# Scores of each batch moved behind its own k_m, the phi softmax one batch ahead, and its quotient folded into k_m and v_m

## Chip, cores and metric

The kernel runs on one core of a Trainium2 chip. The metric is the device time of one execution, in microseconds.

## What is computed

Linear-memory attention over 4 batches, 8 heads, 576 positions and head dimension 64, with 32 memory slots, and then two MLPs over its 2304 x 512 output:

```python
a = exp(phi - max(phi, over s)); a = a / (sum(a, over s) + 1e-9)      # [b,h,s,m]
k_m = einsum('bhsm,bhsd->bhmd', a, k);  v_m = einsum('bhsm,bhsd->bhmd', a, v)
scores = q @ k_m.T / sqrt(64); attn = softmax(scores, over m)
x = attn @ v_m                                       # 2304 x 512
x = (x @ w_a) * (x @ w_b) @ w_out                    # d_ff 1536
out = elu(x @ w_in) @ w2_out                         # d_ff 2048
```

The weights arrive as 64-bit words (float64). They are converted on the chip to a high and a low part, and every large product is done as three products of such parts.

## The kernel before

Everything is written out in program order for each engine (a manual schedule): an engine runs its instructions in the order in which the source emits them, and an instruction that waits holds everything behind it on its engine. SP's DMA queue and POOL's are in order too.

**Attention phase.** One loop over the 4 batches i. phi has 128 partitions (4 heads by 32 slots), two halves u, 576 positions. `a_max` (DVE maximum), `a_exp` (ACT exponential with a running sum) and `a_end` (DVE: add 1e-9, reciprocal, and the product with all of phi, L347) make the softmax over positions. `stage_aT` transposes it on PE into PSUM, and ACT copies it to `a_t` (L366, L369). `stage_kv` (L386) makes k_m (n=0) and v_m (n=1) of one half; `stage_m` (L393) copies the sum out of PSUM on ACT. `stage_turn` (L406) turns k_m and v_m into the layout that is needed next, `stage_kT` and `stage_vT` (ACT, L412, L417) copy that out. `stage_scores` (L426, L430) multiplies q with k_m; `stage_softmax` takes the maximum (L452) and the difference (L453) on DVE and the exponential on ACT (L454); `stage_norm` (L460 to L465, DVE) sums and divides; `stage_xT` (L473, L477) transposes on PE, and `split_sb` writes xhi on ACT (L69) and xlo on DVE (L70).

In iteration i the order is: the four `stage_kv` of batch i, norm of i-2, the end of phi's softmax of i+1, xT of i-2, turn of i, scores of i-1, six conversion pieces, aT of i+1, softmax of i-1, maximum and exponential of phi of i+2. So the scores of a batch run one iteration behind its k_m. The scores of batch 3 stand behind the loop, in the list `order` of the MLP phase, as do the xT of batches 2 and 3.

**Weights.** A unit is 128 x 512 words. `load_unit` brings it to one of three `raw` buffers, from SP's queue where `seq` says "unit", else from POOL's queue inside the third of seven conversion pieces. `magnitude` (L113) and `low_word` (L119) are two ACT passes over the raw unit; the seven pieces of a unit are DVE passes (L160 to L185) with a few ACT copies. `fill(n)` emits n pieces. In piece 4 and 5 of a unit the two ACT passes of the next unit are emitted, and they wait there for its load.

**Loads.** `seq` is the order in which SP loads phi (4 buffers), kv (6), left (2), q (4) and the units. `more_loads` issues from it until a buffer is not free; a stage that has read a buffer frees it and calls it again. k and v come as four transfers of 512 KB for each batch, q and phi as 1152 KB and 576 KB, left as 256 KB.

**MLP phase.** `step_u` (L497) multiplies v_m into w_a and w_b, so the first MLP's input need not be formed; its low part is a DVE pass (L507) deferred by one step. `steps_ab` (L590) multiplies attn with that, DVE multiplies the two results (L599), and ACT and DVE split the product (L600, L601). `steps_o1` (L632) follows, then the second MLP. Every step emits a share of the conversion pieces.

## Time and profile before

| | |
|---|---|
| median of 3 runs | 828.93 us (828.81 to 830.22) |
| the profiled execution | 829.17 us, span 827.4 us |
| PE busy | 790.7 us, 96% of the span |
| DVE busy | 593.1 us, 72% |
| ACT busy | 396.5 us, 48% |
| mean granted clock of TensorE | 0.984 |

The profiled execution's own time is 1.77 us longer than the span from its first to its last instruction. Busy shares are means over stages with different limits. In the views, idle time is put down to what ended it.

### The profile page before, as it was taken

What the parts mean: (1) busy time and instruction counts of PE and PEld (TensorE: products, weight loads), DVE (VectorE), ACT (ScalarE), POOL (GpSimd) and SP (SyncE); (2) the same over time, 40 slices, a digit from 0 to 9 for tenths busy, and PEclk for the clock granted to TensorE, in tenths of its full rate; (3) what the DMA queues carried; (4) which work ended last, traced back from release to release, by engine and by line L of the source; (5) the groups of instructions that cost most, each with busy time, mean ns of one, the idle gap of its engine ahead of it and who ended that gap; (6) DMA issues with size and microseconds to landing.
All of it is one profiled execution on the core that took longest, in us unless ns stands there. A gap on an engine that the chain in (4) does not pass through costs nothing.

```text
span 827.4 us, 14253 instructions
## 1 busy us (share of the span) xinstructions
PE 790.7 (96%) x6032; PEld 729.4 (88%) x6032; DVE 593.1 (72%) x979; ACT 396.5 (48%) x608; POOL 40.5 (5%) x87
## 2 busy tenths in 40 slices
PE   4588899999999999999999999999999999999997
PEld 3477789999999999999999899888999889998896
DVE  3488988678877886667778842787777786776464
ACT  2434576554434433343357754556654556553350
POOL 2000000000000000000000000000000000000000
PEclk9599999999999999999999999999999999999999
DMA  9882022112220221001000200111111110100006
GB/s 325 293 289 102 1 83 97 58 71 78 77 77 27 78 77 51 27 27 51 26 27 26 77 26 15 62 50 35 45 52 51 51 51 26 51 0 1 1 1 229
DMA packets 16815, 57.79 MB, mean 70 GB/s; under 512 B 1776, under 2 KB 1776, under 8 KB 16752
## 3 DMA queue, kind: packets, MB, share of 16 engines
q0 software_dynamic: 9360, 34.08, 11.7%
q1 hardware_dynamic: 7392, 22.81, 7.8%
q8 instruction: 47, 0.77, 0.4%
q14 instruction: 16, 0.13, 0.0%
HBM read 52.17 MB, written 4.72 MB: 69 GB/s over the span
## 4 chain that ended last, share of the span: by engine, by line
PE 91%; DVE 4%; ACT 2%; DMA 2%; issue 0%; SPq 0%; ACTq 0%; DVEq 0%
PE o_ps L776 24%; PE h_ps L733 24%; PE o_ps L632 18%; PE ab_ps L590 18%; PE u_ps L497 2%; PE sc L426 2%; DMA raw<-in_w_ab_dram 1%; PE pk L386 1%; DVE ssm L460 1%; DVE y L465 1%; PE tp_x L473 0%; PE tp_a L362 0%; DVE y L453 0%; DVE smx L452 0%; DMA phi_t<-in_phi_dram 0%
## 5 line engine op out<-in xcount | busy, mean ns | idle before, releaser
L590 PE MATMUL ab_ps<-xhi,u 128*128 128x288 f32 x768 | 139.4, 298 | 3.7 <-ACT xhi L69 2.9
L590 PEld LDWEIGHTS ab_ps<-xhi,u 128*128 128x128 f32 x768 | 114.1, 189 | 9.0 <-issue 3.2
L776 PE MATMUL o_ps<-ulh,g2h 128*128 128x512 f32 x288 | 113.7, 395 | 0.0
L776 PE MATMUL o_ps<-ull,g2h 128*128 128x512 f32 x288 | 113.6, 394 | 0.0
L776 PE MATMUL o_ps<-ulh,g2l 128*128 128x512 f32 x288 | 103.0, 395 | 0.0
L751 DVE SCALAR_TENSOR_TENSOR e<-e,th 128x768 f32<-128x768 f32 x48 | 46.0, 958 | 75.0 <-ACT e L748 74.6
L733 PE MATMUL h_ps<-yh,usl 128*128 128x384 f32 x384 | 97.8, 335 | 0.0
L733 PE MATMUL h_ps<-yl,ush 128*128 128x384 f32 x384 | 97.7, 335 | 0.0
L733 PE MATMUL h_ps<-yh,ush 128*128 128x384 f32 x384 | 97.7, 335 | 0.0
L744 ACT ACTIVATE e<-h_ps 128x768 f32<-128x768 f32 x48 | 39.0, 813 | 95.8 <-PE h_ps L733 93.6
L632 PE MATMUL o_ps<-gh,ulh 128*128 128x288 f32 x384 | 82.5, 296 | 0.6 <-DVE u L507 0.4
L632 PE MATMUL o_ps<-gl,ulh 128*128 128x288 f32 x384 | 82.2, 296 | 0.0
L632 PE MATMUL o_ps<-gh,ull 128*128 128x288 f32 x384 | 82.2, 296 | 0.0
L590 PE MATMUL ab_ps<-xlo,u 128*128 128x288 f32 x384 | 82.1, 295 | 0.0
L597 ACT ACTIVATE a_sb<-ab_ps 128x576 f32<-128x576 f32 x48 | 31.3, 652 | 86.4 <-PE ab_ps L590 86.4
L733 PEld LDWEIGHTS h_ps<-yh,ush 128*128 128x128 f32 x384 | 69.5, 188 | 1.3
L599 DVE TENSOR_TENSOR a_sb<-a_sb,ab_ps 128x576 f32<-128x576 f32 x48 | 36.1, 752 | 46.5 <-PE ab_ps L590 44.8
L733 PEld LDWEIGHTS h_ps<-yh,usl 128*128 128x128 f32 x384 | 69.4, 188 | 0.0
L733 PEld LDWEIGHTS h_ps<-yl,ush 128*128 128x128 f32 x384 | 69.3, 188 | 0.0
L776 PEld LDWEIGHTS o_ps<-ulh,g2l 128*128 128x128 f32 x288 | 54.0, 187 | 13.2
L776 PEld LDWEIGHTS o_ps<-ulh,g2h 128*128 128x128 f32 x288 | 54.0, 187 | 12.6
L776 PEld LDWEIGHTS o_ps<-ull,g2h 128*128 128x128 f32 x288 | 54.0, 187 | 12.5
(93 smaller groups left out, 1338.4 us busy)
## 6 DMA issues: line engine op xcount, KB each, us to landing
raw<-in_w_o_dram POOLq DMA_DIRECT2D x27, 512.0 KB, 3.5
raw<-in_w_ab_dram POOLq DMA_DIRECT2D x22, 512.0 KB, 3.6
kv_t<-in_kv_dram SPq DMA_DIRECT2D x16, 512.0 KB, 10.1
raw<-in_w_i_dram POOLq DMA_DIRECT2D x16, 512.0 KB, 3.6
y<-in_q_dram SPq DMA_DIRECT2D x8, 576.0 KB, 8.8
out_dram<-y SPq DMA_DIRECT2D x8, 512.0 KB, 2.9
phi_t<-in_phi_dram SPq DMA_DIRECT2D x3, 576.0 KB, 11.8
left_t<-in_kv_left_dram SPq DMA_DIRECT2D x4, 256.0 KB, 12.1
```

Of the source, the lines that this page charges most:

```text
L386: nc.tensor.matmul(pk[M * h:M * h + M, D * u:D * u + D], a[0:P if j < NJ else LEFT, u, j, M * h:M * h + M], rows, start=(j == 0), stop=(j ...
L426: nc.tensor.matmul(sc[:, u, j * P:(j + 1) * P], qs[u][:, t, j * P:(j + 1) * P], kt[:, u, t * P:(t + 1) * P], start=(t == 0), stop=(t == 1))
L460: nc.vector.tensor_reduce(out=sm, in_=at, op=ALU.add, axis=AX.X)
L497: nc.tensor.matmul(ps[j:j + M, o, k * 256:k * 256 + 256], vt[r, 2 * k + c, 2 * p + o], w[r, c * 256:c * 256 + 256], start=True, stop=True, ...
L590: nc.tensor.matmul(ps[:, h, 0:HS], u[:, kk, w, n * P:n * P + P], x[b][:, kk, h * HS:(h + 1) * HS], start=(kk == 0 and i == 0), stop=(kk == ...
L597: nc.scalar.activation(out=a_sb, in_=ps[:, :, 0:HS], func=AF.Copy)
L599: nc.vector.tensor_tensor(out=a_sb, in0=a_sb, in1=ps[:, :, 0:HS], op=ALU.mult)
L632: nc.tensor.matmul(ps[:, h, 0:HS], w[:, cc], g[:, h * HS:(h + 1) * HS], start=(n == 0 and i == 0), stop=(n == len(fs) - 1 and i == 2),)
L733: nc.tensor.matmul(ps[:, h, 0:HB], w[:, c], x[:, c, h * HB:(h + 1) * HB], start=(c == 0 and i == 0), stop=(c == KC - 1 and i == 2),)
L744: nc.scalar.activation(out=e, in_=ps[:, :, 0:HB], func=AF.Relu, scale=-1.0)
L751: nc.vector.scalar_tensor_tensor(out=e, in0=e, scalar=1.0, in1=th, op0=ALU.add, op1=ALU.mult)
L776: nc.tensor.matmul(ps[:, k, :], g[:, c * P:(c + 1) * P], w, start=(f == fs[0] and i == 0), stop=(f == fs[-1] and i == 2),)
```

## The change

Batch i's scores now run in iteration i, behind its own turn, with aT of i+1 (or the first `step_u`) on PE between the turn and the scores. phi's maximum, exponential and reciprocal of batch i+2 are done in iteration i. The product with all of phi is gone; the reciprocal is instead the scale of the ACT copy that takes k_m and v_m out of PSUM, which becomes two copies of 64 columns each. The exponential of the scores is a stage of its own, emitted one iteration later, behind the first `stage_m`; norm and xT of i-1 run in iteration i. The list `order` loses the scores of batch 3, and some of its entries change places. The two ACT passes of a unit are emitted right ahead of its first piece until iteration 1 is over, and only then one unit ahead. Conversion pieces are emitted as 7 in iteration 0 (behind `stage_vT`), and 7 in each of the iterations 1 to 3 (ahead of norm). In `seq`, q of a batch now follows its own kv and the phi ahead of it, and precedes the kv of the next batch.

```diff
@@ -93,7 +93,7 @@
...
     live = {False: 0, True: 0}
-    state = {"loaded": 0, "n": 0, "slot": 0}
+    state = {"loaded": 0, "n": 0, "slot": 0, "ahead": False}
     def load_unit(eng=nc.gpsimd):
         n = state["loaded"]
@@ -108,13 +108,13 @@
     def magnitude(n):
-        if n < NU:
+        if n < NU and "a" not in cu[n]:
             a = conv.tile([P, 512], U32, tag="a", name="a", bufs=2)
             nc.scalar.activation(out=a.bitcast(F32), in_=cu[n]["h"].bitcast(F32), func=AF.Abs, scale=65536.0)
             cu[n]["a"] = a
     def low_word(n):
-        if n < NU:
+        if n < NU and "lw" not in cu[n]:
             t = conv.tile([P, 512], BF16, tag="lw", name="lw", bufs=2)
             nc.scalar.activation(out=t, in_=cu[n]["l"], func=AF.Copy, scale=2.0 ** -52)
             cu[n]["lw"] = t
@@ -150,6 +150,9 @@
...
         whole = n < NU
+        if whole and slot == 0:
+            magnitude(n)
+            low_word(n)
         a = cu[n]["a"] if whole else None
         if slot == 1 and not to_hi(n - 1):
             return False
@@ -173,10 +176,12 @@
...
             cu[n]["p2"] = p2
-            low_word(n + 1)
+            if state["ahead"]:
+                low_word(n + 1)
         elif whole and slot == 5:
             nc.vector.tensor_tensor(out=cu[n]["lw"], in0=cu[n]["lw"], in1=cu[n]["p2"], op=ALU.mult)
-            magnitude(n + 1)
+            if state["ahead"]:
+                magnitude(n + 1)
         elif whole and slot == 6:
             to = a.bitcast(F32)
             if whole_words(n):
@@ -210,7 +215,7 @@
...
-    FILLS = 6, 6, 6, 6
+    FILLS, FILLS2 = (0, 7, 7, 7), (0, 0, 0, 0)
     RATE_AB, RATE_U, RATE_O1 = 1.0, 1.0, 3.0
     RATE_H, RATE_O2 = 2.5, 3.0
     ORDER, ORDER_H, ORDER_O2 = "0f1a2", "fa0bf1c2", "0f1fa2"
@@ -305,14 +310,12 @@
     NPHI, NQ, NKV = 4, 4, 6
-    seq = [("phi", 0, (0,)), ("phi", 0, (1,)), ("left", 0), ("kv", 0, 1, 0), ("kv", 0, 1, 1),
-           ("kv", 0, 0, 0), ("kv", 0, 0, 1), ("unit",), ("phi", 1)]
-    for b in range(1, B):
+    seq = [("phi", 0, (0,)), ("phi", 0, (1,))]
+    for b in range(B):
         seq += [("left", b)] + [("kv", b, n, u) for n in (1, 0) for u in range(2)]
         seq += [("unit",)] if b < 3 else []
-        seq += [("phi", b + 1)] if b + 1 < B else []
-        seq += [("q", b - 1, 0), ("q", b - 1, 1)]
-    seq += [("q", B - 1, 0), ("q", B - 1, 1)]
+        seq += [("phi", x) for x in ((1, 2), (3,), (), ())[b]]
+        seq += [("q", b, 0), ("q", b, 1)]
     free = {"phi": NPHI, "q": NQ, "kv": NKV, "left": 2}
     loads = {"phi": load_phi, "q": load_q, "kv": load_kv, "left": load_left, "unit": lambda: load_unit(nc.sync)}
@@ -336,20 +339,14 @@
     def a_exp(b, u):
         t = st["phi", b][:, u]
-        sm = p0.tile([P, 1], F32, tag="sm", name="sm", bufs=3)
+        sm = p0.tile([P, 1], F32, tag="sm", name="sm", bufs=4)
         nc.scalar.activation(out=t, in_=t, func=AF.Exp, bias=st.pop(("nm", b, u)), accum_out=sm)
         st["sm", b, u] = sm
     def a_end(b, u):
-        t, sm = st["phi", b][:, u], st.pop(("sm", b, u))
+        sm = st["sm", b, u]
         nc.vector.tensor_scalar(out=sm, in0=sm, scalar1=1e-9, scalar2=None, op0=ALU.add)
         nc.vector.reciprocal(out=sm, in_=sm)
-        nc.vector.tensor_scalar(out=t, in0=t, scalar1=sm, scalar2=None, op0=ALU.mult)
...
-    def stage_a(b, u):
-        a_max(b, u)
-        a_exp(b, u)
-        a_end(b, u)
     def stage_aT(b, us=(0, 1)):
         t = st["phi", b]
@@ -390,7 +387,9 @@
     def stage_m(b, n):
         t = st["m", n, b] = p0.tile([P, 2, D], F32, tag="m", name="m", bufs=2)
-        nc.scalar.activation(out=t, in_=st.pop(("pk", n, b))[:, 0:2 * D].rearrange("p (u d) -> p u d", u=2), func=AF.Copy)
+        pk = st.pop(("pk", n, b))
+        for u in range(2):
+            nc.scalar.activation(out=t[:, u], in_=pk[:, D * u:D * u + D], func=AF.Copy, scale=st["sm", b, u])
     def stage_turn(b, n):
@@ -451,7 +450,11 @@
...
             nc.vector.tensor_tensor(out=at, in0=ps, in1=mx.to_broadcast(list(at.shape)), op=ALU.subtract)
-            nc.scalar.activation(out=at, in_=at, func=AF.Exp, scale=SCALE)
...
+    def stage_exp(b):
...
+        for (at, _, _), n in zip(st["at", b], (P, LEFT)):
+            nc.scalar.activation(out=at[0:n], in_=at[0:n], func=AF.Exp, scale=SCALE)
     def stage_norm(b):
@@ -522,57 +525,61 @@
...
         more_loads()
-        stage_a(0, 0)
-        stage_aT(0, (0,))
-        stage_a(0, 1)
-        stage_aT(0, (1,))
-        magnitude(0)
-        low_word(0)
-        fill(2)
+        for u in range(2):
+            a_max(0, u)
+            a_exp(0, u)
+            stage_aT(0, (u,))
+        for u in range(2):
+            a_end(0, u)
         for i in range(B):
...
                 stage_m(i, n)
-            if i == 0:
-                fill(4)
-                a_max(1, 0)
-                a_max(1, 1)
-                a_exp(1, 0)
-                a_exp(1, 1)
-            if i > 1:
-                stage_norm(i - 2)
-            if i + 1 < B:
-                a_end(i + 1, 0)
-                a_end(i + 1, 1)
-            if i == B - 1:
-                step_u(0, 0, 0)
+                if n and i:
+                    stage_exp(i - 1)
+            fill(FILLS[i])
+            if i:
+                stage_norm(i - 1)
+            else:
+                for u in range(2):
+                    a_max(1, u)
+                    a_exp(1, u)
+                for u in range(2):
+                    a_end(1, u)
             tick()
-            if i > 1:
-                stage_xT(i - 2)
             stage_turn(i, 1)
             stage_turn(i, 0)
             stage_kT(i)
             stage_vT(i)
-            if i == B - 1:
+            if i == 0:
+                magnitude(0)
+                low_word(0)
+                fill(7)
+            if i + 1 < B:
+                stage_aT(i + 1)
+            else:
                 es_l.close()
                 es_p.close()
                 pb = es_b.enter_context(tc.tile_pool(name="pb", bufs=2, side="right", reuse_waits="tile"))
                 pss.append(ctx.enter_context(tc.tile_pool(name="ps2", bufs=2, space=PSUM, reuse_waits="tile")))
-            if i:
-                stage_scores(i - 1)
-            fill(FILLS[i])
-            if i + 1 < B:
-                stage_aT(i + 1)
-            if i:
-                soft_tiles(i - 1)
-                stage_softmax(i - 1)
-            if i + 2 < B:
-                a_max(i + 2, 0)
-                a_max(i + 2, 1)
-                a_exp(i + 2, 0)
-                a_exp(i + 2, 1)
+                step_u(0, 0, 0)
+            stage_scores(i)
+            tick()
+            for u in range(2 if i + 2 < B else 0):
+                a_max(i + 2, u)
+                a_exp(i + 2, u)
+            fill(FILLS2[i])
+            soft_tiles(i)
+            stage_softmax(i)
+            for u in range(2 if i + 2 < B else 0):
+                a_end(i + 2, u)
+            state["ahead"] = i > 0
+            if i and i + 1 < B:
+                stage_xT(i - 1)
+        stage_exp(B - 1)
...
         def steps_ab(f, b, amount):
             u = u_t.pop((f, b))
             a_sb = pb.tile([P, 2, HS], F32, tag="a_sb", name="a_sb", bufs=3)
@@ -657,15 +664,8 @@
...
-        def last_scores():
-            stage_norm(last - 1)
-            stage_scores(last)
-            soft_tiles(last)
-            stage_softmax(last)
...
-        order = [("ab", 0, 0), ("do", last_scores), ("ab", 0, 1), ("u", 1, 0), ("u", 0, 1),
-                 ("do", lambda: stage_xT(last - 1)), ("ab", 1, 0), ("do", lambda: stage_norm(last)), ("ab", 0, 2),
+        order = [("ab", 0, 0), ("do", lambda: stage_xT(last - 1)), ("u", 1, 0), ("ab", 0, 1), ("u", 0, 1),
+                 ("do", lambda: stage_norm(last)), ("ab", 1, 0), ("ab", 0, 2),
                  ("do", lambda: stage_xT(last)), ("ab", 1, 1), ("u", 1, 1), ("ab", 0, 3), ("ab", 1, 2),
                  ("u", 2, 0), ("u", 2, 1), ("ab", 1, 3)]
         for f in range(2, NF1):
```

## Rows read from the trace of the kernel before

**Rows 1.** Windows by stage: busy us of each engine, PEclk granted clock, DMA share, GB/s.

```profile
18.84:29.69 10.85, 0.00 (x1) 0.00 (x1) 3.00 (x8) 2.95 (x9) 0.53 (x1) 0.55 1.03 378
45.60:75.87 30.27, 25.03 (x513) 20.95 (x513) 26.44 (x49) 14.28 (x31) 0.53 (x1) 1.00 0.57 194
75.87:113.28 37.41, 33.42 (x325) 30.79 (x325) 33.35 (x57) 18.58 (x30) 1.59 (x3) 1.00 0.09 29
145.00:827.40 682.40, 677.83 (x4472) 630.17 (x4470) 488.24 (x785) 326.42 (x462) 29.48 (x53) 1.00 0.14 49
```

**Rows 2.** Chain that ended last, 0 to 30 us: start, us, what.

```profile
14.49 12.22 DMA raw<-in_w_ab_dram
```

**Rows 3.** Timeline of ACT: start us, us, engine, line, op, out<-in [idle before <-releaser].

```profile
26.74 0.66 ACT L119 ACTIVATE lw<-raw 128x512 bf16<-128x512 uint32 x1 [8.77 <-DMA raw<-in_w_ab_dram]
...
27.84 0.76 ACT L340 ACTIVATE phi_t<-phi_t,nm 128x576 f32<-128x576 f32 x1
...
38.54 0.28 ACT L393 ACTIVATE m<-pk 128x128 f32<-128x128 f32 x1 [2.48 <-PE pk L386]
...
86.21 1.36 ACT L454 ACTIVATE y<-y 128x1024 f32<-128x1024 f32 x2 [6.84 <-DVE y L453]
```

**Rows 4.** Timeline of PE, same columns.

```profile
18.20 0.64 PE L406 MATMUL pt<-y,m 128*64 128x128 f32 x8
29.69 1.97 PE L362 MATMUL tp_a<-ident,phi_t 128*128 128x128 f32 x8 [10.85 <-DVE sm L345]
...
39.92 5.65 PE L426 MATMUL sc<-y 128*128 128x128 f32 x32
...
48.79 0.65 PE L386 MATMUL pk<-kv_t,a_t 128*32 128x64 f32 x32 [0.95 <-ACT a_t L366]
...
53.59 1.07 PE L473 MATMUL tp_x<-ident,y 128*128 128x128 f32 x8 [1.42 <-DVE y L465]
...
55.67 3.84 PE L426 MATMUL sc<-y 128*128 128x128 f32 x32
...
60.46 1.09 PE L362 MATMUL tp_a<-ident,phi_t 128*128 128x128 f32 x8
...
75.87 0.53 PE L590 MATMUL ab_ps<-xhi,u 128*128 128x288 f32 x2
...
79.17 3.73 PE L426 MATMUL sc<-y 128*128 128x128 f32 x32
...
93.41 0.50 PE L590 MATMUL ab_ps<-xhi,u 128*128 128x288 f32 x2 [2.92 <-ACT xhi L69]
```

**Rows 5.** Timeline of SP's queue: start us, us, line, transfer issued.

```profile
4.29 0.61 SPq L103 DMA_DIRECT2D raw<-in_w_ab_dram  x1
...
19.32 0.34 SPq L293 DMA_DIRECT2D y<-in_q_dram  x1
```

**Rows 6.** DMA issues at 4.29 and 19.32 us: KB, us from issue to landing.

```profile
raw<-in_w_ab_dram SPq DMA_DIRECT2D x1, 512.0 KB, 12.1
...
y<-in_q_dram SPq DMA_DIRECT2D x1, 576.0 KB, 13.2
```

**Rows 7.** Timeline of DVE, columns as in rows 3.

```profile
29.93 0.52 DVE L347 TENSOR_SCALAR phi_t<-phi_t,sm 128x576 f32<-128x576 f32 x1
...
70.94 0.68 DVE L168 SCALAR_TENSOR_TENSOR a<-raw,a 128x512 uint32<-128x512 uint32 x1
...
73.65 0.43 DVE L163 TENSOR_SCALAR a<-a 128x512 uint32<-128x512 uint32 x1
...
80.11 1.53 DVE L460 TENSOR_REDUCE ssm<-y 128x32 f32<-128x1024 f32 x2
...
83.71 1.21 DVE L452 TENSOR_REDUCE smx<-sc 128x32 f32<-128x1024 f32 x1
...
86.88 0.41 DVE L173 TENSOR_SCALAR p<-a 128x512 uint16<-128x512 uint16 x1
...
93.19 1.23 DVE L70 TENSOR_TENSOR xlo<-tp_x,xhi 128x1024 fp32r<-128x1024 f32 x1
```

## The prediction

> **What bounds the kernel now.** I read the windows by stage first [rows 1]. From 145 us to the end PE is busy 677.83 of 682.40 us, so nothing there can give much; the change must be judged in the first 113.28 us, up to the first product of `steps_o1`. Between 75.87 and 113.28 us PE is busy 33.42 of 37.41 us. The large hole is 18.84 to 29.69 us: PE does nothing, and TensorE's granted clock falls.

> The chain of waits names the hole [rows 2]: the raw unit that SP issued at 14.49 us lands 12.22 us later. The timeline of ACT shows why weights stop the attention [rows 3]: the `low_word` of unit 1 waits for that unit until 26.74, and the exponentials of phi(1) at 27.84 stand behind it in ACT's queue. PE starts aT(1) at 29.69 and finds the clock at half: scores(0) take 5.65 us on L426, scores(1) only 3.84 [rows 4].

> The DMA is full meanwhile (share 1.03) [rows 1], so what comes next is the landing of the data. Unit 0, the 3392nd KB of SP's order, lands at 4.29 + 12.1 = 16.4 us, and q(0)'s second half, the 8512th (KB of 1024 bytes), at 19.32 + 13.2 = 32.5 [rows 5, 6]. With one unit of POOL's between them that is (8512 - 3392 + 512) / 16.1 = 350 KB/us.

> **The change: reference point.** All work from the first o1 product on is the same in both kernels. So the new time is 829.17 - (113.28 - T1), where T1 is when PE gets there now. I follow PE, with each wait that could be last.

> **Loads, new order.** From 16.4 us and KB 3392 at 350 KB/us: phi(1) 18.1, phi(2) 19.7, q(0) 23.0, the four kv(1) 25.2 to 29.6, unit 1 31.0, phi(3) 32.7, q(1) 36.0, kv(2) 38.2 to 42.6, unit 3 44.1; one POOL unit (1.5 us more), q(2) 48.9, kv(3) to 55.5; another POOL unit, q(3) 60.3. SP issues some 12 us ahead, and the buffers that it waits for (kv, left, q) come free earlier than that, so I take the DMA as never starved. Bounds: the mean up to unit 0 is (3392 + 512) / 14.4 = 271 KB/us, which puts q(3) at 16.4 + 15296 / 271 = 72.8; the upper end is the hole's 378 GB/s, 369 KB/us [rows 1], q(3) at 57.9.

> **Batch 0.** Without L347 (0.52 us each on DVE [rows 7]) aT(0) starts a little earlier. This saving I cost at nothing: phi(1) lands at 18.1 anyway. Its two maxima and two exponentials, with the 1.9 us from the first exponential to PE [rows 3, 4], put aT(1) at about 20. PE has then been idle some 3 us and I take the low clock: aT 2.5 us, to 22.6. q(0) is there at 23. Scores at the half clock for 4 us (before, they rose to the full clock after about 4 us of L426), then full: to 28.9 us.

> **Batch 1.** kv at full clock takes 53.59 - 1.42 - 48.79 = 3.4 us [rows 4]; the last kv(1) is needed at 31.5 and lands at 29.6. So to 32.3. `stage_m` is now two copies with a scale, which the trace does not show; one 128-column copy takes 0.28 us [rows 3], so two halves lie between 0.28 and 0.56; I take 0.44, nearer to two fixed costs; the extra 0.16 counts four times between kv and turn, 0.6 us. [...]

> From here DVE is the tightest engine. Prices [rows 7]: six pieces of a unit 3.2 us (70.94 to 73.65, and 0.43), norm 3.6 (80.11 to 83.71), the DVE part of softmax 3.2 (83.71 to 86.88), xlo 1.35, two maxima 1.3, the rest of `a_end` 0.75. Pieces of unit 1 start when ACT has made its magnitude, behind m(1,0), at 33.5: to 36.7; norm(0) 40.3; maxima of phi(3) 41.6; softmax(1) 44.8; `a_end` 45.5; xlo(0) 46.9. On PE meanwhile turn and aT(2) to 34.9, scores(1) to 39.8 (q(1) 36.0 is in time), xT(0) waits for norm(0), 40.3 to 41.7, kv(2) to 45.1.

> **Batches 2 and 3.** DVE: pieces of unit 2 to 50.0, norm(1) 53.6. PE: turn to 46.9, aT(3) 48.2; kT(2) is behind four conversion passes on ACT, 48.7; scores(2) 48.9 to 53.8 with q(2); xT(1) to 55.2; kv(3), with the last transfer at 55.5, to 58.7. ACT's m, two passes, kT and vT to 61.5; `step_u` 62.5; scores(3) (4.8 us from first product to the next stage [rows 4]) 62.5 to 67.4. DVE's pieces, norm(2) and u's low part end near 66.5, so softmax(3) follows at once, to 70. I take 68 for the first `steps_ab`, rounded up for waits of some tenths that I did not count.

> **To T1.** Before, from 75.87: 33.42 us of PE work [rows 1], of which scores(3), here already done, are 4.7; 28.7 remain. Before there are 3.99 us of idle: 2.92 of it is PE at 93.41 waiting for xhi, because ACT had stood 6.84 us at the exponential of batch 3 [rows 3, 4]. In the new order that exponential is before the phase, so that stall goes. What is late next: the low part of the second `step_u` is deferred by one step and is now emitted behind norm(3). DVE runs from 70 through pieces, L599, xlo(2), two low parts and norm(3) to about 83.7 and gives that low part at 85.9; PE, with 3.3 us for each `steps_ab` (75.87 to 79.17 [rows 4]), wants it at 82.2. That is a stall of 3.7 us; bounds 0 (DVE less late) and 6. T1 = 68 + 28.7 + 3.7 = 100.4.

> **Sum.** 829.17 - (113.28 - 100.4) = 816.3 us in the profiled execution's terms; the median of the runs was 0.24 lower, so **816 us**.

> **Rivals.**
> *The clock stays low longer.* For: at 18.84 PE idle brings it down, and between 29.69 and 39.92 us the aT and kv products did not bring it back. Against: it stays full through later gaps of 1 to 1.5 us [rows 1, 4]. Low through kv(1) and scores(1) adds 2.2 + 0.7 + 1.9, about 5 us: 821. [...]

> *The loads set the end.* With 271 KB/us scores(3) start at 72.8 instead of 62.5: 826. This is also the way to **slower**: q(b) is now needed in its own iteration, where before it had a batch of slack. From scores(3) starting at 75.9 us on, that is below 15296 / 59.5 = 257 KB/us, the kernel is slower than before; at 240 it is 833. Against: the hole's rate is 378 GB/s with all queues full [rows 1].

> *More is won.* The clock is back early in scores(0) (2 us) and DVE gives the low part in time (3.7 us): 810.5.

> *It does nothing.* What is won is given back because DVE, busy 33.35 of 37.41 us before T1 [rows 1], holds PE in the first MLP: 829. For it speaks that conversions are only shifted; against it, that DVE loses L347 and stood idle 7.85 of the hole's 10.85 us, so that there is room for its work to move forward.

> **How the numbers follow.** A measurement here tells about 0.2% (1.7 us). Forecast 0.62 (811 to 821); low clock or slow loads, still faster, 0.17 (821 to 827); more won 0.12; nothing 0.03; slower 0.06. The range 810 to 824 leaves out a third of the second (above 824), half of the third (below 810) and the last two, together 0.2. Faster 0.91, same 0.03, slower 0.06.

> **What would show it.** The wait of ACT for the raw unit near 14 to 27 us is gone, and PE has no hole over 4 us after aT(1). The last q lands near 60 us; the first `steps_ab` starts near 68, the first o1 product near 100. DVE has next to no idle from 33 to 70 us. A stall on `ab_ps` behind norm(3), put down to DVE's L507, near 82 us. From T1 on the two timelines run the same. I am wrong if q(2), q(3) or kv(3) land more than 5 us late, if the granted clock stays at half beyond 30 us, or if PE's idle after T1 grows by more than 2 us.

## The result, and the profile after

The changed kernel took 815.45 us (median of 4 runs, 814.24 to 816.64), the kernel before 828.87 us beside it (4 runs, 827.61 to 830.22): a ratio of 0.9838, with a 95% interval of 0.9812 to 0.9863. The forecast was 816 us, range 810 to 824. The profiled execution took 816.60 us, with a span of 814.8.

The windows of the changed kernel come first, for four stretches (columns as in [rows 1]).

```profile
0.00:30.00 30.00, 17.01 (x346) 13.28 (x347) 12.16 (x28) 13.24 (x32) 5.12 (x23) 1.00 0.96 346
...
30.20:36.00 5.80, 5.80 (x77) 4.72 (x77) 2.31 (x5) 2.35 (x8) 0.34 (x1) 0.50 1.03 307
...
48.32:84.13 35.81, 31.71 (x458) 26.99 (x457) 34.42 (x62) 18.59 (x36) 1.58 (x3) 1.00 0.31 120
...
100.63:814.80 714.17, 708.44 (x4794) 658.32 (x4792) 518.57 (x837) 349.35 (x513) 32.54 (x59) 1.00 0.15 51
```

From the first o1 product on nothing changed: 714.17 us here, 827.4 - 113.28 = 714.12 before [rows 1, 4]. So the whole gain lies ahead of that product, which moved from 113.28 to 100.63 us. The chain of waits no longer holds a weight unit of 12.22 us, as in [rows 2]; at its start now stands the second half of q(0), issued at 7.64 us and landed 14.09 us later, for which PE waits 0.66 us. What PE waited for in all is this (the view of waits; us in total, times, longest):

```profile
PE tp_a L359 <- ACT phi_t L343: 9.2, 3, 5.9
PE pk L383 <- issue: 4.1, 2, 2.8
PE ab_ps L597 <- DVE u L510: 3.0, 2, 2.7
PE o_ps L639 <- DVE u L510: 1.6, 1, 1.6
PE sc L425 <- ACT y L411: 0.8, 1, 0.8
PE sc L425 <- DMA y<-in_q_dram: 0.7, 1, 0.7
```

The hole of 10.85 us ahead of aT(1) [rows 4] has become 1.87. The second entry is new: "issue" means that PE waited for nothing that the profile shows. The timeline of PE says where it was:

```profile
17.32 1.42 PE L359 MATMUL tp_a<-ident,phi_t 128*128 128x128 f32 x8 [1.87 <-ACT phi_t L343]
...
21.87 2.02 PE L425 MATMUL sc<-y 128*128 128x128 f32 x16 [0.66 <-DMA y<-in_q_dram]
...
26.73 0.65 PE L383 MATMUL pk<-kv_t,a_t 128*32 128x64 f32 x30 [0.16 <-PE pk L383]
30.19 0.37 PE L383 MATMUL pk<-kv_t,a_t 128*32 128x64 f32 x2 [2.82 <-issue]
...
35.98 4.04 PE L425 MATMUL sc<-y 128*128 128x128 f32 x32
...
46.34 0.55 PE L383 MATMUL pk<-kv_t,a_t 128*32 128x64 f32 x25 [1.27 <-issue]
...
47.07 0.45 PE L405 MATMUL pt<-pair,m 128*64 128x64 f32 x8
...
50.26 3.84 PE L425 MATMUL sc<-y 128*128 128x128 f32 x32 [0.79 <-ACT y L411]
...
66.65 0.53 PE L597 MATMUL ab_ps<-xhi,u 128*128 128x288 f32 x2
...
84.18 1.16 PE L597 MATMUL ab_ps<-xhi,u 128*128 128x288 f32 x4 [2.68 <-DVE u L510]
...
100.63 0.43 PE L639 MATMUL o_ps<-gh,ulh 128*128 128x288 f32 x2
```

The first of these holes splits a group of 32 products of one tile, whose data were there, into 30 and 2, the second one into 7 and 25. DVE, by its timeline:

```profile
33.48 0.43 DVE L163 TENSOR_SCALAR a<-a 128x512 f32<-128x512 f32 x1 [5.79 <-ACT a L113]
...
48.32 0.43 DVE L163 TENSOR_SCALAR a<-a 128x512 f32<-128x512 f32 x1 [1.60 <-ACT a L113]
...
67.62 1.21 DVE L451 TENSOR_REDUCE smx<-sc 128x32 f32<-128x1024 f32 x1
...
82.92 1.21 DVE L510 TENSOR_TENSOR u<-u_ps,u 128x1024 fp32r<-128x1024 f32 x1
```

From 48.32 us, the first piece of unit 2, to 84.13, the end of u's low part, DVE is busy 34.42 of 35.81 us. PE's stall ends 0.05 us behind it.

### The profile page after: what moved, and what is told of

The parts are those of the page before. It is cut to its first block, busy times and chain, and to the rows that moved or that the text cites. A ratio compares the mean times of both kernels' runs of the same rounds, so it can differ in the third digit from the quotient of the medians.

```text
span 814.8 us, 14254 instructions
## 1 busy us (share of the span) xinstructions
PE 790.4 (97%) x6032; PEld 728.1 (89%) x6032; DVE 589.4 (72%) x971; ACT 398.7 (49%) x616; POOL 40.3 (5%) x87
## 4 chain that ended last, share of the span: by engine, by line
PE 91%; DVE 4%; DMA 2%; ACT 1%; issue 1%; SPq 0%; DVEq 0%
PE o_ps L776 25%; PE h_ps L733 25%; PE o_ps L639 19%; PE ab_ps L597 18%; PE u_ps L500 2%; DMA y<-in_q_dram 2%; PE pk L383 1%; PE sc L425 1%; DMA kv_t<-in_kv_dram 1%; DVE u L510 0%; DVE y L468 0%; DVE ssm L463 0%; DVE y L452 0%; DVE smx L451 0%; DVE gl L608 0%
## 5 line engine op out<-in xcount | busy, mean ns | idle before, releaser
L606 DVE TENSOR_TENSOR a_sb<-a_sb,ab_ps 128x576 f32<-128x576 f32 x48 | 36.1, 753 | 47.3 <-PE ab_ps L597 46.9
L776 PEld LDWEIGHTS o_ps<-ulh,g2l 128*128 128x128 f32 x288 | 54.0, 187 | 13.2
L776 PEld LDWEIGHTS o_ps<-ulh,g2h 128*128 128x128 f32 x288 | 54.0, 187 | 12.7
## 6 DMA issues: line engine op xcount, KB each, us to landing
raw<-in_w_ab_dram SPq DMA_DIRECT2D x3, 512.0 KB, 12.3
```

Of the source, the lines that this page charges most:

```text
L606: nc.vector.tensor_tensor(out=a_sb, in0=a_sb, in1=ps[:, :, 0:HS], op=ALU.mult)
L776: nc.tensor.matmul(ps[:, k, :], g[:, c * P:(c + 1) * P], w, start=(f == fs[0] and i == 0), stop=(f == fs[-1] and i == 2),)
```

## The experiments

My theory: the weight passes and the load order win the start of the phase together, and from then on DVE's chain sets T1. The rival: PE's own chain, with its clock and its holes, or the loads set T1 all along. X stands for the start of unit 2's first piece on DVE (48.32 in the changed kernel).

**b_unit_late**: the kernel before, with the two ACT passes of a unit emitted late until iteration 1 is over, and the six conversion pieces of iteration 0 behind aT(1).

```diff
...
+        if whole and slot == 0:
+            magnitude(n)
+            low_word(n)
...
-            fill(FILLS[i])
+            if i:
+                fill(FILLS[i])
             if i + 1 < B:
                 stage_aT(i + 1)
+            if i == 0:
+                fill(FILLS[i])
+            state["ahead"] = i > 0
```

> The kernel before, with one thing changed: in iterations 0 and 1 the two ACT passes over a raw unit stand right ahead of its first piece, and iteration 0's six pieces behind aT(1), so no exponential of phi stands behind a unit's load. Theory 'the unit's wait is the first of several limits': the exponentials of phi(1) run near 19 to 20 us and kv(1) ends near 32 instead of 38.4, but scores(0) then wait for q(0), which lands at 32.5 in this load order; about 6 of the 10.85 us come out, 822 to 823.5 us. Rival 'the wait was the whole loss': all 10 us come out, 818 to 819. Rival 'the hole only moves': 828 to 829.

Measured: 825.45 us (823.85 to 828.61, 10 runs) beside 829.25, ratio 0.9963 (0.9949 to 0.9978). aT(1) starts at 20.21 and the first o1 product at 107.91 in the profiled execution. The weights did stop the attention, but freeing it alone gives about 4 us (5.4 at the first o1 product of the profiled execution, the fastest of the ten), less than the 6 us that the theory expected.

**b_fold**: the kernel before, with the quotient folded into `stage_m` (and more buffers for the sums `sm`).

```diff
...
-        nc.vector.tensor_scalar(out=t, in0=t, scalar1=sm, scalar2=None, op0=ALU.mult)
...
+        for u in range(2):
+            nc.scalar.activation(out=t[:, u], in_=pk[:, D * u:D * u + D], func=AF.Copy, scale=st["sm", b, u])
```

> The kernel before with the fold alone: no product with phi on DVE (8 times 0.52 us), the reciprocal as scale of two 64-column copies. Theory: hidden, since the unit's load still sets when PE goes on; three later batches lose up to 0.5 us of DVE each and gain 0.24 us of ACT each (two copies 0.52 us against 0.28): 827.5 to 829.5. Rival 'the fold is the gain': 8 times 0.52 us on the path, 825 or less.

Measured: 828.62 us (828.14 to 831.76, 10 runs), ratio 0.9994 (0.9985 to 1.0004). PE still stands 10.29 us ahead of aT(1). The fold alone is worth nothing there. What it is worth in the new order was not run: of the products that it saves, those with phi(2) and phi(3) would fall into stretches where DVE waits anyway (5.79 and 1.60 us, ahead of 33.48 and 48.32 us), but that is argued.

**a_old_loads**: the changed kernel with the old list of loads.

```diff
-    seq = [("phi", 0, (0,)), ("phi", 0, (1,))]
-    for b in range(B):
+    seq = [("phi", 0, (0,)), ("phi", 0, (1,)), ("left", 0), ("kv", 0, 1, 0), ("kv", 0, 1, 1),
+           ("kv", 0, 0, 0), ("kv", 0, 0, 1), ("unit",), ("phi", 1)]
+    for b in range(1, B):
...
+        seq += [("q", b - 1, 0), ("q", b - 1, 1)]
+    seq += [("q", B - 1, 0), ("q", B - 1, 1)]
```

> The changed kernel with the old list of loads alone. Theory 'the order of the loads is needed by the new order of the stages': scores(0) cannot start before q(0)'s landing near 32 us (19.2 and 21.9 with the new list), later q's stand behind kv transfers that wait for buffers; the first steps_ab start near 74 to 77 instead of 66.65, 822 to 826 us. Unit 0 lands again near 16.4 us, not 14.1, if what is queued behind it (left(1)) slows it. Rival 'DVE sets the pace anyway': 815 to 817.

Measured: 830.49 us (828.71 to 833.23, 10 runs), ratio 1.0023 (1.0010 to 1.0036): slower than before, 15 us above the changed kernel, and beyond the 822 to 826 us that the theory expected. The timeline of SP's queue shows why (start, us, transfers issued):

```profile
17.18 1.83 SPq L298 DMA_DIRECT2D y<-in_q_dram  x2
...
21.00 15.38 SPq L308 DMA_DIRECT2D kv_t<-in_kv_dram  x4
...
37.38 0.90 SPq L298 DMA_DIRECT2D y<-in_q_dram  x2
...
38.89 18.78 SPq L308 DMA_DIRECT2D kv_t<-in_kv_dram  x4
57.72 1.95 SPq L298 DMA_DIRECT2D y<-in_q_dram  x4
```

The timeline of PE in the same execution:

```profile
27.81 5.74 PE L427 MATMUL sc<-y 128*128 128x128 f32 x32 [6.53 <-DMA y<-in_q_dram]
...
46.70 3.75 PE L427 MATMUL sc<-y 128*128 128x128 f32 x16 [6.48 <-DVE nm L339]
...
64.26 3.81 PE L427 MATMUL sc<-y 128*128 128x128 f32 x32 [2.74 <-DMA y<-in_q_dram]
```

Scores(0) wait 6.53 us for q(0), which stands behind the four kv(1) in the old list and is issued only at 17.18 (at 6.58 with the new list). PE cannot read kv(1) before these scores, and a kv buffer comes free only when PE has read it: so the four kv(2) take 15.38 us to issue, where they took this long with the new list:

```profile
25.34 4.93 SPq L308 DMA_DIRECT2D kv_t<-in_kv_dram  x4
```

q(1) and q(2) stand behind kv(2) and kv(3) in the same queue, and scores(1) and scores(2) wait for them 6.48 and 2.74 us (the first is listed under a maximum that DVE had done by 27.7 us; q(1), issued at 37.38, landed 9.2 us later). The new place of the scores thus needs the new list: without it, the change loses what the weight passes won. The new list without the new place was not run.

**a_norm_late** and **norm_late_again**: the changed kernel with the norm of batch 3 one step later, first beside the kernel before, then beside the changed kernel.

```diff
-                 ("do", lambda: stage_norm(last)), ("ab", 1, 0), ("ab", 0, 2),
+                 ("ab", 1, 0), ("do", lambda: stage_norm(last)), ("ab", 0, 2),
```

> The changed kernel with norm(3) emitted behind steps_ab(1,0) instead of ahead of it. Theory: the 2.68 us that PE waits for u's low part behind norm(3), and the half clock from 84.2 to 87.4 us that follows it (about 1.4 us), go; xT(3) may wait up to 1 us for norm(3): 811.5 to 813.5. Rival 'DVE is the bound and the wait only moves': 815 to 816.5.

> The changed kernel with the norm of batch 3 behind the first steps_ab of half 1 once more, now beside the changed kernel itself. If the stall of 2.68 us on u's low part is on the path that sets the end, it is about 2 us faster than the changed kernel (813.4 against 815.5). If the difference seen before was the scatter of the early phase, it is under 1 us.

Measured: 813.35 us (812.33 to 815.12, 4 runs), ratio 0.9809 (0.9793 to 0.9825), and again 812.63 us (812.19 to 812.96, 4 runs), ratio 0.9800 (0.9786 to 0.9815). The stall on u's low part is gone, and PE waits at xT(3) for the norm instead (timeline of PE in norm_late_again; 1.43 us in a_norm_late):

```profile
84.23 1.06 PE L476 MATMUL tp_x<-ident,y 128*128 128x128 f32 x8 [1.42 <-DVE y L468]
```

This version is faster than both kernels. In the profiled executions X to T1 took 50.19 and 49.45 us, where the changed kernel took 52.31 and, in the run that follows, 51.00. X came at 47.20 and 46.95 us, up to 1.4 us sooner than in the changed kernel; the edit lies behind X, so that part is not shown to be its work.

**after_again**: the changed kernel once more.

> The changed kernel once more, as the reference for the three kernels beside it on the same chip. Every theory expects 814.2 to 816.6 us. The question is only how far the time and the first product of steps_ab scatter when nothing is changed.

Measured: 817.43 us (814.78 to 818.78, 4 runs), ratio 0.9854 (0.9831 to 0.9877). So the eight runs of the changed kernel lie between 814.24 and 818.78, wider than expected. All four of norm_late_again, on the same chip, lie below. The timeline of PE in the profiled execution, which is the fastest of these four, shows one source of the spread; what made the others slower is not known:

```profile
83.93 0.80 PE L597 MATMUL ab_ps<-xhi,u 128*128 128x288 f32 x4 [2.69 <-DVE u L510]
...
84.83 0.69 PE L597 MATMUL ab_ps<-xhi,u 128*128 128x288 f32 x4
...
98.83 0.43 PE L639 MATMUL o_ps<-gh,ulh 128*128 128x288 f32 x2
```

The same stall (2.69 us) is followed by the full clock, and T1 comes 14.90 us behind it. In the first profile the granted clock was 0.53 from 84.2 to 87.4 us, four products took 1.16 instead of 0.69, and T1 came 16.45 us behind. Of the seven profiled executions that have this stall, T1 comes 14.9 us behind its end in three and 16.2 to 16.5 in four. So the stall costs its 2.7 us and, in some executions, some 1.5 more.

**a_order**: as a_norm_late, and the second `step_u` of half 1 and its `steps_ab` ahead of xT(3).

```diff
-                 ("do", lambda: stage_norm(last)), ("ab", 1, 0), ("ab", 0, 2),
-                 ("do", lambda: stage_xT(last)), ("ab", 1, 1), ("u", 1, 1), ("ab", 0, 3), ("ab", 1, 2),
+                 ("ab", 1, 0), ("do", lambda: stage_norm(last)), ("ab", 0, 2), ("u", 1, 1), ("ab", 1, 1),
+                 ("do", lambda: stage_xT(last)), ("ab", 1, 2), ("ab", 0, 3),
```

> The changed kernel with norm(3) behind steps_ab(1,0), as in the run before, and in addition step_u(1,1) and steps_ab(1,1) ahead of xT(3) and steps_ab(1,2) behind it, so that PE has 7.6 us of work between norm(3)'s emission and xT(3). Theory: the 1.43 us that PE waited for norm(3) at xT(3) go: 811 to 813 us, 0.980 or less of the kernel before. Rival 'the wait moves to the next place': 813 to 814.5, no better than the run with norm(3) moved alone.

Measured: 813.46 us (812.39 to 813.93, 4 runs), ratio 0.9814 (0.9796 to 0.9831). The wait moved, now 1.54 us for u's low part at 90.41, and the time is that of a_norm_late.

**a_dve_more**: the row maxima of the scores of batches 1 and 2 taken twice, which is 1.62 us more of DVE's work in each of iterations 1 and 2.

```diff
-            nc.vector.tensor_reduce(out=mx, in_=ps, op=ALU.max, axis=AX.X)
+            for _ in range(2 if b in (1, 2) else 1):
+                nc.vector.tensor_reduce(out=mx, in_=ps, op=ALU.max, axis=AX.X)
```

> The row maxima of the scores of batches 1 and 2 are taken twice: 1.21 + 0.41 = 1.62 us more of DVE work in each of iterations 1 and 2, the result unchanged. If DVE sets the start of the first steps_ab, that start moves by 2 x 1.62 = 3.2 us and the time from 815.5 to about 818.7. If PE sets it, neither moves by more than 0.5 us. In between if the two hand over to each other.

Measured: 818.03 us (815.39 to 818.93, 4 runs), ratio 0.9855 (0.9837 to 0.9873); the runs overlap those of after_again, so the trace must tell. The timeline of DVE:

```profile
49.26 0.43 DVE L163 TENSOR_SCALAR a<-a 128x512 f32<-128x512 f32 x1 [0.75 <-ACT a L113]
...
62.31 0.41 DVE L163 TENSOR_SCALAR a<-a 128x512 f32<-128x512 f32 x1
```

The timeline of PE in the same kernel:

```profile
47.28 0.55 PE L383 MATMUL pk<-kv_t,a_t 128*32 128x64 f32 x25 [2.92 <-issue]
...
86.76 1.33 PE L598 MATMUL ab_ps<-xhi,u 128*128 128x288 f32 x4 [2.69 <-DVE u L511]
```

The first addition vanishes in DVE's wait ahead of X (0.75 us instead of 1.60; X itself is 0.94 later because PE's hole is 2.92 us instead of 1.27). The second shows in full: from X to the end of the stall it is 86.76 - 49.26 = 37.50 us, where the changed kernel has 84.18 - 48.32 = 35.86, so 1.64 more for 1.62 added. Behind X DVE sets the time, ahead of it not.

**a_pe_more**: the transposes of phi of batches 2 and 3 done twice.

```diff
-        for u in us:
+        for u in list(us) * (2 if b > 1 else 1):
             for j in range(NJ):
                 nc.tensor.transpose(tp[:, u, j * P:(j + 1) * P], t[:, u, j * P:(j + 1) * P], ident)
```

> The transposes of phi of batches 2 and 3 are done twice: eight more 128x128 transposes, 1.1 us at the full clock and 2.0 at half, of PE work in each of iterations 1 and 2, the result unchanged. If DVE sets the start of the first steps_ab, the time stays within 0.5 us of 815.5. If PE sets it, that start moves by 2.2 to 3.1 us and the time to 817.7 to 818.6.

Measured: 815.79 us (815.08 to 816.76, 4 runs), ratio 0.9839 (0.9825 to 0.9854), no more than the changed kernel. X is 48.36, the stall ends at 84.20 and T1 is 99.12. PE's additions are hidden: that of aT(3) in PE's wait for kT(2), that of aT(2) by the clock, which fell later behind the hole and was back sooner (32 kv products took 0.65 us behind the hole, not 1.08, and scores(1) 3.74 us, not 4.04).

**a_shift**: the last turn of batch 0 done four times, so that PE's later instructions all stand 24 products further on.

```diff
-            stage_turn(i, 0)
+            stage_turn(i, 0, 4 if i == 0 else 1)
```

> The changed kernel with the last turn of batch 0 done four times instead of once, which puts 24 more rows of PE ahead of everything later, in a gap in which PE waits for phi(1) anyway. In the changed kernel PE stands 2.82 us at 27.37 us, within one stage_kv, ahead of its 347th product row, and 1.27 us ahead of the 600th. Theory 'PE waits for its own instructions, which come over the full DMA': the holes stay at the 347th and 600th row counted from the start, so that they lie 24 rows earlier in the work: between the 6th and 7th row of the third stage_kv of batch 1, and 24 rows ahead of the old place in batch 2. Rival 'PE waits for k, v or left': they stay at the same products of the work, 30 rows into the third stage_kv. Time within 1.5 us of the changed kernel.

Measured: 816.69 us (one execution). There is no hole near the 347th product, where the theory expected one, and the second is now this, by the timeline of PE:

```profile
42.21 0.54 PE L383 MATMUL pk<-kv_t,a_t 128*32 128x64 f32 x23
44.59 0.48 PE L383 MATMUL pk<-kv_t,a_t 128*32 128x64 f32 x9 [1.84 <-issue]
```

In the changed kernel it stood behind 7 products of the fourth call of `stage_kv` of batch 2 (three calls of 40, and 7), here behind 23 of the third (80 and 23): 24 earlier in the work. a_pe_more, with 8 more products ahead of it, has the hole 8 products earlier, behind the 39th of the third call. The hole follows the number of the instruction and not the data.

**a_few_loads**: q, k and v of batches 1 to 3 are constants written by GpSimd and not loaded, so the output is that of other inputs.

```diff
-        nc.sync.dma_start(out=t, in_=q[b][:, 2 * u:2 * u + 2])
+        if b:
+            nc.gpsimd.memset(t, 0.01)
+        else:
+            nc.sync.dma_start(out=t, in_=q[b][:, 2 * u:2 * u + 2])
...
-        nc.sync.dma_start(out=t, in_=kv[b, n, u])
+        if b:
+            nc.gpsimd.memset(t, 0.01)
+        else:
+            nc.sync.dma_start(out=t, in_=kv[b, n, u])
```

> The changed kernel with q, k and v of the batches 1 to 3 set to a constant on GpSimd instead of loaded (the output is that of other inputs): SP moves 5.7 of 17.3 MB and the DMA is idle from about 25 us on. Theory 'the full DMA costs the changed kernel the holes, and unit 1's landing at 29.8': no hole above 1 us at the 347th and 600th row, the DVE chain of pieces, norm and softmax starts near 28 to 30 instead of 33.5 us, and the first o1 product comes at 93 to 97 instead of 100.6: 809 to 812.5 us. Rival 'DVE alone sets it': 814 to 816.5. Rival 'the loads are most of it': 805 or less.

Measured: 814.95 us (814.06 to 815.85, 2 runs), ratio 0.9833 (0.9810 to 0.9855). Without these 3 x 3200 KB of loads the time is the same, and T1 is 99.47, not the 93 to 97 that the theory expected. The hole at the 347th product shrinks to 0.50 us and that at the 600th is not there (0.61 us of "issue" stand at 49.00), but X is still 47.06, with DVE's norm late (PE waits 1.94 us for it at 38.90). What the loads alone allow is not shown, since a pass of DVE's took 0.94 us longer beside these writes (last section).

## Why the prediction was right, step by step

**Reference point.** T1 was forecast at 100.4 and measured at 100.63; behind it both kernels take the same time to 0.05 us. The sum of the prediction is confirmed there, but its terms less well, and the closeness is in part luck: the first `steps_ab` came 1.35 us sooner than forecast, the stall was 1.02 us shorter, and the rest of the way to T1 took 31.30 us, not 28.7.

**Loads.** Somewhat early: phi(1) landed at 15.6 us (forecast 18.1), unit 1 landed at 17.53 + 12.3 = 29.8 (forecast 31.0), the two q(3), issued from 44.19 us, about 12.7 us behind their issue, the last near 58.5 (60.3). Unit 0 landed at 4.33 + 9.8 = 14.1, where [rows 5, 6] gave 16.4. That the DMA never starves held in the new order (its share is 1.00 to 1.05 in each stretch of 2 us from 10 to 52 us), and no scores waited more than 0.66 us for q; a_old_loads shows that the order itself decides this, which the prediction had only as a risk of the rate.

**Batch 0 and 1.** Errors that cancelled. With phi(1) aT(1) came sooner, at 17.32 and not about 20. The half clock forecast for aT(1) and scores(0) hardly came: after a gap of 1.87 us aT took 1.42 and scores(0) ran at 2.02 for 16 products, so that they ended at 24.9 and not 28.9. Against that stood a hole of 2.82 us in kv(1) that no step had, and the half clock (a granted 0.50) from 30.2 to 36.0 us behind it, with PE busy throughout. So unit 1's pieces started at 33.48, where 33.5 was forecast. In after_again the errors fall the other way (5.51 us for scores(0), no hole near the 347th product) and the pieces start at 31.99. How fast PE is clocked so early must be read from the products: the granted clock of the rows is 1.00 there, but it is 1.00 too where 32 kv products took 1.08 us (9.84 us in the changed kernel), as they did at 0.50 behind the hole (30.86 us).

**The fold and the m pair.** The fold was costed at nothing in batch 0, and b_fold shows nothing. The pair of copies was forecast at 0.44 us and measured at 0.52, near the bound of 0.56: 0.3 us over the four.

**DVE as the tightest engine.** Right from X on, and so were the prices: from X to the end of softmax(3) on DVE it is 70.78 - 48.32 = 22.46 us, where 70 - 46.9 = 23.1 was forecast. X itself was forecast at 46.9 out of DVE's chain, and measured at 48.32, because DVE waited 1.60 us for ACT's magnitude behind m(2,0), and so for PE: its kv(2) ended at 47.1 and not 45.1, behind the second hole. The first `steps_ab` at 66.65 (forecast 68) did not matter for T1, since DVE's low part at 84.13 set what followed.

**The stall.** The place and the cause were right. The low part was ready at 84.13 (forecast 85.9), PE wanted it at 81.50 (82.2): 2.68 us instead of 3.7. Not forecast was that the clock can fall behind it, worth 1.5 us of the rest in the first profile: together 4.2.

**The rivals.** "The loads set the end" does not describe this kernel; a_old_loads is that rival, by another mechanism: not a low rate but the order of the queue, and a queue that stands. "The clock stays low longer" came in part. Half the clock beyond 30 us, which the prediction named as a sign of being wrong, did show (30.2 to 36.0 us), but behind a hole that it did not have; scores(1) took 4.04 us, nearly the full clock's 3.84 [rows 4], and X was late by 1.4 us, not by 5. Where scores(0) took 5.51 us instead (after_again), X was 47.83, no later. That gaps of 1 to 1.5 us leave the clock full held here (second hole, 1.27 us, with a granted 1.00 behind it) and not in after_again: there the clock fell in the second hole, of 1.21 us, and stood at 0.50 from 45.4 to 51 us. "It does nothing" fell: DVE is as busy behind X as that rival supposes, and T1 still came 12.65 us sooner. My theory that DVE sets all from unit 1's pieces on fell: a_dve_more limits it to what lies behind X, and ahead of X PE and what it waits for decide. "More is won" is what a_norm_late does: 2.1 us less in its first runs, 4.8 beside after_again, scatter ahead of X included.

## What to carry to other kernels

When a consumer is moved ahead in the work, move its load ahead in the queue with it, and look for buffers that come free only by work which waits for something behind them in that queue. Add a known piece of work to each engine in turn: the one where it shows in full, and from which point on, is the bound there. Sums over a startup phase can come out right with wrong terms, so compare the steps and not only the end.

## What the runs showed of the hardware

**PE's holes by instruction count.** In the changed kernel PE stood still behind its 346th and 599th product, and a_norm_late behind its 599th and 852nd, always 253 apart. b_unit_late, in which no scores stand ahead of the kv products of batch 1, has a hole of 0.98 us behind its 346th too, 30 products into the fourth call of `stage_kv` of that batch, where the changed kernel is 30 into the third. The windows up to each hole of a_norm_late:

```profile
0.00:44.48 44.48, 33.25 (x599) 26.99 (x600) 24.18 (x53) 20.81 (x51) 5.67 (x24) 0.92 0.98 338
0.00:58.30 58.30, 45.47 (x852) 37.17 (x852) 35.65 (x73) 27.91 (x67) 6.20 (x25) 0.94 0.98 337
```

Of the holes in the timelines above the longest is that of 2.92 us in a_dve_more. During the first one of the changed kernel the DMA is full and carries a packet of a queue that the view of the DMA calls "instruction" (27.4 to 28.4 us):

```profile
q1 hardware_dynamic: 102, 0.42, 103.2%
q8 instruction: 1, 0.02, 6.8%
```

**GpSimd beside DVE.** In a_few_loads one piece of a conversion (128 x 512) took 1.37 us at 31.22 while GpSimd wrote constants, and 0.43 us otherwise. It is one record, and other passes of DVE's beside such writes took no longer than before (1.23 us for a difference 128x1024 at 41.58, as in the changed kernel); the cause is not shown.
